# A new order table for the instructions of a fused linear-attention and MoE kernel

## The chip, the cores and the metric

The kernel runs on one core of one Trainium2 chip. The metric is device time in microseconds (us), the median of several executions. Engines: TensorE (PE; its weight loads are PEld), VectorE (DVE), ScalarE (ACT), GpSimd (POOL) and SyncE (SP), which issues all DMA transfers of this kernel.

## The reference

First a linear attention with a complex decay per channel, of which the real part goes on (4 batches, 8 heads, 768 steps, head size 48):

```
mag = np.sqrt(a_re * a_re + a_im * a_im)
scale = np.minimum(mag, 0.999) / (mag + 1e-06)
a_re_n, a_im_n = (a_re * scale, a_im * scale)
...
for t in range(S):
    ar, ai = (a_re_n[:, :, t, :, None], a_im_n[:, :, t, :, None])
    new_re = ar * S_re - ai * S_im
    new_im = ar * S_im + ai * S_re
    kv = np.einsum('bhd,bhe->bhde', k[:, :, t], v[:, :, t])
    S_re, S_im = (new_re + kv, new_im)
    y[:, :, t] = np.einsum('bhd,bhde->bhe', q[:, :, t], S_re)
```

Then, with `x` of shape (4, 768, 384) made of `y`, a gated feed-forward layer of width 1024 with a convolution of three steps:

```
h = np.maximum(x @ w_in, 0.0)
...
for k in range(K):
    conv_out += conv_w[k][None, None, :] * hp[:, k:k + S, :]
gate = 1.0 / (1.0 + np.exp(-conv_out))
return (h * gate @ w_out).astype(np.float32)
```

## The kernel before

The sequence of each batch is cut into three **segments** of two **chunks** of 128 steps, so there are 12 segments (0 to 11) and 24 chunks. The weights come in first, in eight pieces through the buffers `stk` (L278), are put together on VectorE (L248 to L251) and split into a rounded part and a rest (L281 to L287).

For each segment `prelude` loads the decay (`a_t`, L306) and works out logarithms, scans and phases on ScalarE and VectorE (L309 to L337). `products` loads `qk_t` (L345) and `v_t` (L355), takes exponentials and sines on ScalarE (L347, L348, L358, L359), and multiplies on VectorE: L349 and L350, then L360 and L361 into `qk_t`, and L362 into `a_t`. Then SyncE issues 16 DMA copies of 96 KB (L367): eight `stk<-qk_t` and eight `stk<-a_t`, one for each head, which bring real and imaginary part of a head together on 96 partitions.

For each chunk `state` turns `qk_t` (L386, L387) and adds to the running state (L393, L400), and `attention` multiplies the copies with each other in 16 matmuls (L415, in two halves), masks each half on VectorE (L419, `p_t<-ps`), and multiplies with state and values (L434, `ps<-p_t,v_t`). ScalarE takes the result (L446), VectorE the rest (L447).

The feed-forward layer works on units of 256 or 384 steps, four steps `f2` each. `moe_front`: matmul L500, ScalarE L503, VectorE L504 and L506. `moe_back`: ScalarE L518, VectorE L519, ScalarE L521, VectorE L522, matmul L527, and at a unit's end ScalarE L533 and the store L534. ScalarE's function tables are loaded where neighbouring functions need other sets (L190). A last check of the value ranges decides on a slow path, which isn't taken.

Buffers matter for loads: `a_t` has 3, `qk_t` 2, `v_t` 3 and `stk` 4, and a load or copy into a buffer waits until its last reader is done.

What sets the order: each engine executes its own list in order, and waits where an instruction's inputs or its buffer aren't ready. The lists come from the table `RANKS`, one number for each piece of work; `in_order` sorts the pieces by it and chains each engine's list. SyncE's list is the one queue in which all transfers are issued.

```
rows = pieces(list(nc.cur_bb.bb.instructions))
...
for k in sorted(range(len(rows)), key=lambda k: RANKS[k]):
    lines.setdefault(str(rows[k][0].engine), []).append(rows[k])
```

Of the kernel before, what the change touches and what calls it, by code (L numbers as in the profile page):

```python
# [47 lines left out]
    8, 13, 0, 5, 12, 11, 15, 3, 26, 7, 9, 14, 1, 4, 6, 0, 11, 21, 30, 53, 55, 69,  # L48
    72, 73, 83, 74, 82, 1, 1, 2, 3, 7, 0, 1, 9, 2, 3, 16, 3, 4, 5, 12, 14, 4,
    6, 20, 5, 9, 26, 4, 7, 8, 18, 22, 7, 8, 29, 10, 11, 34, 7, 13, 17, 20, 24, 12,  # L50
    16, 41, 13, 17, 39, 8, 25, 26, 33, 38, 18, 19, 48, 20, 21, 57, 9, 28, 31, 32, 55, 25,
    29, 67, 28, 30, 68, 13, 43, 44, 46, 70, 35, 37, 72, 36, 38, 73, 14, 45, 48, 60, 71, 40,
    48, 88, 43, 44, 91, 0, 2, 1, 0, 3, 5, 4, 6, 8, 11, 6, 11, 14, 15, 23, 10, 9,
    16, 10, 17, 19, 25, 21, 5, 18, 32, 24, 34, 6, 17, 27, 28, 27, 29, 35, 18, 16, 15, 19,
    28, 26, 25, 30, 29, 23, 24, 31, 20, 22, 21, 32, 14, 43, 15, 45, 24, 63, 22, 51, 23, 52,
    26, 2, 10, 59, 58, 27, 64, 31, 62, 32, 69, 33, 64, 34, 67, 39, 41, 78, 75, 2, 12, 19,
    23, 13, 15, 31, 33, 35, 36, 22, 36, 38, 37, 42, 30, 39, 41, 40, 46, 42, 50, 51, 12, 47,
    56, 49, 59, 27, 38, 52, 54, 54, 56, 61, 34, 47, 39, 41, 37, 35, 40, 48, 44, 49, 46, 45,
    50, 43, 42, 51, 42, 79, 45, 83, 52, 95, 46, 78, 47, 79, 49, 50, 87, 81, 102, 109, 89, 92,
    51, 98, 53, 97, 59, 107, 57, 90, 58, 92, 60, 61, 106, 98, 54, 96, 88, 96, 55, 100, 99, 101,  # L60
    56, 104, 95, 107, 62, 110, 109, 116, 64, 114, 102, 106, 66, 116, 104, 111, 121, 122, 112, 127, 115, 76,
    77, 82, 84, 67, 128, 117, 119, 68, 132, 125, 127, 130, 135, 120, 138, 123, 83, 88, 85, 92, 126, 124,
    121, 145, 131, 89, 95, 91, 97, 141, 151, 139, 155, 144, 100, 98, 103, 99, 170, 108, 172, 92, 10, 37,
    44, 50, 40, 49, 58, 60, 65, 66, 47, 62, 66, 65, 80, 53, 57, 63, 68, 76, 71, 90, 84, 36,
    77, 82, 77, 80, 52, 55, 86, 93, 84, 85, 87, 57, 60, 58, 56, 71, 66, 61, 62, 64, 70, 68,
    65, 59, 69, 67, 63, 63, 115, 65, 120, 73, 133, 69, 108, 70, 110, 71, 72, 16, 18, 125, 114, 158,
    169, 129, 131, 74, 118, 75, 122, 80, 81, 160, 147, 78, 142, 132, 137, 79, 144, 130, 134, 87, 148, 135,
    143, 90, 152, 141, 150, 93, 156, 145, 157, 94, 161, 146, 151, 154, 150, 148, 164, 152, 111, 109, 112, 114,
    96, 167, 158, 165, 102, 174, 161, 163, 162, 168, 154, 177, 159, 113, 115, 130, 126, 110, 183, 171, 187, 117,
    190, 178, 183, 178, 171, 167, 193, 177, 133, 128, 134, 132, 118, 196, 179, 184, 124, 200, 190, 191, 187, 185,  # L70
    169, 203, 188, 135, 136, 145, 147, 223, 116, 229, 137, 127, 204, 203, 205, 131, 216, 201, 211, 217, 220, 198,
    228, 207, 153, 154, 155, 157, 137, 225, 217, 229, 143, 238, 223, 224, 218, 226, 206, 232, 212, 156, 158, 163,
    160, 234, 241, 216, 247, 227, 168, 167, 172, 170, 256, 255, 232, 260, 236, 173, 181, 180, 187, 276, 156, 284,
    141, 33, 61, 74, 70, 75, 81, 85, 99, 103, 101, 76, 93, 94, 97, 111, 94, 89, 91, 86, 123, 113,
    134, 137, 53, 113, 117, 103, 105, 78, 93, 139, 140, 124, 126, 128, 73, 86, 74, 79, 75, 80, 82, 84,
    83, 85, 89, 77, 90, 87, 76, 88, 86, 157, 101, 166, 106, 180, 104, 155, 105, 156, 107, 17, 20, 181,
    164, 108, 179, 116, 189, 121, 211, 119, 172, 120, 173, 122, 123, 195, 175, 54, 105, 112, 100, 108, 118, 119,
    143, 147, 146, 129, 136, 138, 133, 159, 153, 149, 142, 140, 165, 153, 173, 175, 81, 163, 176, 162, 160, 96,
    110, 182, 184, 166, 168, 174, 98, 97, 104, 113, 95, 99, 105, 94, 102, 101, 107, 111, 109, 112, 106, 103,
    125, 207, 129, 202, 140, 215, 138, 192, 139, 193, 141, 142, 219, 197, 144, 222, 146, 224, 150, 264, 148, 202,  # L80
    149, 204, 151, 152, 19, 21, 231, 210, 252, 239, 236, 237, 159, 243, 220, 225, 161, 246, 226, 237, 165, 249,
    231, 234, 166, 254, 233, 235, 169, 262, 240, 246, 171, 263, 245, 247, 266, 268, 243, 274, 253, 186, 192, 194,
    190, 195, 196, 179, 280, 264, 275, 188, 288, 267, 282, 270, 269, 251, 282, 260, 191, 201, 203, 204, 202, 205,
    277, 278, 256, 292, 273, 208, 206, 207, 215, 216, 228, 310, 316, 290, 322, 295, 225, 226, 230, 227, 234, 231,
    329, 178, 338, 197, 341, 189, 72, 136, 188, 170, 149, 192, 191, 194, 198, 199, 176, 181, 180, 182, 205, 213,
    196, 194, 195, 221, 200, 233, 227, 100, 208, 212, 189, 214, 115, 134, 230, 240, 213, 215, 218, 121, 131, 127,
# [641 lines left out]
```

## Time and profile before

| | us |
|---|---|
| three timed executions | 421.44, 417.04, 418.19 |
| their median | 418.19 |
| the profiled execution | 414.24 |
| its span, from the first to the last instruction | 412.5 |
| busy in the span: TensorE, VectorE, ScalarE | 352.3, 326.5, 333.9 |

The rows further down come from the profiled execution, which was 3.95 us faster than the median of the timed ones. Times in rows count from the start of the span. Of the busy time of TensorE, the ends of matmuls are modelled.

### The profile page before, as it was taken

The numbers are of one execution on the slowest core, as the hardware profiler recorded it, in microseconds if no ns is written. First come the engines' busy times: TensorE is split into PE (matmuls) and PEld (weight loads), VectorE is DVE, ScalarE is ACT, GpSimd is POOL, SyncE is SP. The second block draws the span as 40 slices with busy tenths as digits, with TensorE's granted clock in tenths as the row PEclk, the third lists the DMA queues.
The fourth block names the chain that finished last, engine by engine and source line by source line (L and its number), as shares of the span: only waits on it lengthen the run. The fifth ranks groups of instructions, "written<-read, shape, count | busy, mean of one in ns | idle before, by whom it ended". The sixth has DMA issues, their size and how long they took to land.

```text
span 412.5 us, 12055 instructions
## 1 busy us (share of the span) xinstructions
PE 352.3 (85%) x5106; PEld 321.5 (78%) x5106; DVE 326.5 (79%) x515; ACT 333.9 (81%) x574; POOL 4.3 (1%) x35
## 2 busy tenths in 40 slices
PE   0566387979998979999989889799989899999993
PEld 0233365868987979998978889799979799999992
DVE  2889896669997879998998779849979778484670
ACT  5999989579998989999999979949989765453450
POOL 3000000000000000000000000000000000000000
PEclk9999798799999999999999999969999999999997
DMA  8995768284385775484768735823737533900001
GB/s 312 367 366 119 168 196 184 89 237 116 39 230 163 195 178 205 75 191 121 209 158 225 201 110 84 235 81 60 209 82 167 128 121 65 195 27 2 36 24 65
DMA packets 33231, 62.24 MB, mean 151 GB/s; under 512 B 4496, under 2 KB 26000, under 8 KB 33168
## 3 DMA queue, kind: packets, MB, share of 16 engines
q1 hardware_dynamic: 33168, 61.38, 55.5%
q8 instruction: 42, 0.69, 0.7%
q14 instruction: 21, 0.17, 0.1%
HBM read 37.77 MB, written 4.72 MB: 103 GB/s over the span
## 4 chain that ended last, share of the span: by engine, by line
PE 44%; DMA 20%; ACT 18%; DVE 6%; SPq 6%; issue 3%; ACTq 0%; DVEq 0%
PE o L527 14%; PE h_ps L500 11%; PE ps L415 7%; PE ps L434 7%; DMA qk_t<-in_qk 6%; DMA stk<-a_t 5%; DMA stk<-qk_t 5%; SPq L367 4%; ACT L190 3%; DMA v_t<-in_v 3%; PE s_ps L393 2%; PE ps L386 2%; DMA a_t<-in_a 1%; PE h_ps L285 1%; ACT h_t L503 1%
## 5 line engine op out<-in xcount | busy, mean ns | idle before, releaser
L527 PE MATMUL o<-wo,hg 128*128 128x384 f32 x576 | 116.2, 343 | 1.0 <-issue 0.8
L500 PE MATMUL h_ps<-x,wi 128*128 128x386 f32 (+1 forms) x648 | 113.0, 323 | 1.2 <-issue 1.2
L500 PEld LDWEIGHTS h_ps<-x,wi 128*128 128x128 f32 x648 | 104.0, 189 | 2.5 <-issue 1.8
L527 PEld LDWEIGHTS o<-wo,hg 128*128 128x128 f32 x576 | 98.4, 188 | 3.9 <-issue 1.2
L415 PE MATMUL ps<-stk 96*64 96x64 f32 (+1 forms) x768 | 46.0, 263 | 22.2 <-DMA stk<-a_t 9.7
L415 PEld LDWEIGHTS ps<-stk 96*64 96x64 f32 x768 | 40.0, 145 | 30.1 <-issue 10.1
L419 DVE TENSOR_TENSOR p_t<-ps,mask 128x384 f32<-128x384 f32 x48 | 26.4, 553 | 28.9 <-PE ps L415 28.2
L504 DVE SCALAR_TENSOR_TENSOR g_t<-h_t,cw 128x384 f32<-128x384 f32 (+1 forms) x72 | 40.0, 566 | 8.4 <-ACT h_t L503 8.0
L190 ACT ACT_TABLE_LOAD x36 | 46.2, 1283 | 0.6
L518 ACT ACTIVATE g_t<-g_t,cw 128x384 f32<-128x384 f32 (+1 forms) x72 | 40.0, 574 | 5.4 <-DVE g_t L506 5.3
L503 ACT ACTIVATE h_t<-h_ps 128x386 f32<-128x386 f32 (+1 forms) x72 | 31.8, 448 | 15.0 <-PE h_ps L500 15.0
L506 DVE SCALAR_TENSOR_TENSOR g_t<-h_t,cw,g_t 128x384 f32<-128x384 f32 (+1 forms) x72 | 39.9, 565 | 0.4
L285 PE MATMUL h_ps<-g_t,ident 128*128 128x384 f32 x32 | 19.9, 719 | 22.3 <-DVE g_t L251 15.0
L522 DVE TENSOR_TENSOR hg<-g_t,hg 128x768 fp32r<-128x768 f32 (+1 forms) x36 | 31.0, 861 | 5.4 <-ACT hg L521 5.4
L519 DVE SCALAR_TENSOR_TENSOR g_t<-g_t,h_t 128x768 f32<-128x768 f32 (+1 forms) x36 | 31.0, 862 | 2.0 <-ACT g_t L518 1.8
L521 ACT ACTIVATE hg<-g_t 128x768 fp32r<-128x768 f32 (+1 forms) x36 | 27.7, 769 | 5.4 <-DVE g_t L519 4.7
L434 PE MATMUL ps<-p_t,v_t 128*32 128x64 f32 x1344 | 26.9, 227 | 4.7 <-issue 4.7
L446 ACT ACTIVATE x<-ps 128x384 fp32r<-128x384 f32 x24 | 11.7, 489 | 23.6 <-PE ps L434 23.4
L434 PEld LDWEIGHTS ps<-p_t,v_t 128*32 128x32 f32 x1344 | 24.6, 115 | 6.4 <-issue 6.2
L285 PEld LDWEIGHTS h_ps<-g_t,ident 128*128 128x128 f32 x32 | 6.7, 255 | 29.1 <-issue 15.7
L434 PE MATMUL ps<-stk,s_sb 96*32 96x128 f32 x640 | 23.5, 290 | 0.1
L387 ACT COPY kn<-ps 128x512 f32<-128x512 f32 (+1 forms) x40 | 19.8, 499 | 3.8 <-PE ps L386 3.5
(93 smaller groups left out, 496.1 us busy)
## 6 DMA issues: line engine op xcount, KB each, us to landing
v_t<-in_v SPq DMA_DIRECT2D x24, 512.0 KB, 5.1
a_t<-in_a SPq DMA_DIRECT2D x12, 768.0 KB, 5.2
qk_t<-in_qk SPq DMA_DIRECT2D x12, 768.0 KB, 6.6
stk<-qk_t SPq DMA_DIRECT2D x96, 96.0 KB, 3.7
stk<-a_t SPq DMA_DIRECT2D x96, 96.0 KB, 3.7
out<-os_t SPq DMA_DIRECT2D x24, 192.0 KB, 2.8
stk<-in_w_in SPq DMA_DIRECT2D x4, 768.0 KB, 9.8
stk<-in_w_out SPq DMA_DIRECT2D x4, 768.0 KB, 6.6
```

Of the source, the lines that this page charges most:

```text
L190: row = [nc.scalar.preload_act_table_set(min(loads[k])).ins, *row]
L285: nc.tensor.matmul(rest, lhsT=ident, rhs=tmp[:, cut], start=True, stop=False)
L415: nc.tensor.matmul(sp[r0:r0 + HC, i, to], lhsT=stk[0][:, h, lo:lo + HC], rhs=stk[1][:, h, lo:], start=(i == 0 and lo == 0), stop=(i == 1 a ...
L434: nc.tensor.matmul(yp[r0:r0 + 32, q // 4, t0:t0 + right.shape[-1]], lhsT=left, rhs=right, start=r0 not in started, stop=n >= len(jobs) - H ...
L500: nc.tensor.matmul(hp, lhsT=wi[:, f2, iw, i, kt], rhs=x[ix][:, kt], start=(k == 0), stop=(k == 8))
L503: nc.scalar.activation(h, hp, func=AF.Relu)
L504: nc.vector.scalar_tensor_tensor(out=g, in0=h[:, 0:n], scalar=cw[:, f, 0:1], in1=h[:, 1:n + 1], op0=ALU.mult, op1=ALU.add)
L506: nc.vector.scalar_tensor_tensor(out=g, in0=h[:, 2:n + 2], scalar=cw[:, f, 2:3], in1=g, op0=ALU.mult, op1=ALU.add)
L518: nc.scalar.activation(g[:, i], g[:, i], func=AF.Tanh, scale=cw[:, 2 * f2 + i, 1:2])
L519: nc.vector.scalar_tensor_tensor(out=g, in0=g, scalar=1.0, in1=h[:, :, 1:n + 1], op0=ALU.add, op1=ALU.mult)
L522: nc.vector.tensor_tensor(out=lo, in0=g, in1=hi.bitcast(F32), op=ALU.subtract)
L527: nc.tensor.matmul(ops[t], lhsT=hg[:, k, t * C:(t + 1) * C], rhs=wo[:, f2, w, k], start=(f2 == 0 and hg is hi and k == 0 and w == 0), stop ...
```

## The change

Only the numbers of `RANKS` change. All 1793 pieces of work stay, with the same operands and the same buffers, but each engine's list stands in a new order. The one instruction that comes is a table load on ScalarE, which follows from the order there. The table has 82 lines; all change, and the first shows as much as any:

```
 RANKS = [
-    8, 13, 0, 5, 12, 11, 15, 3, 26, 7, 9, 14, 1, 4, 6, 0, 11, 21, 30, 53, 55, 69,
...
+    2, 10, 0, 3, 7, 8, 12, 14, 15, 6, 5, 16, 9, 0, 4, 13, 1, 0, 11, 27, 41, 58,
```

What the new numbers do is seen in the lists. A row is a line of the program, the operation, the output and the inputs (with buffer numbers), and the output's shape.

VectorE in segment 8, whose decay is `a_t_3583`: the rows up to the two L419 of its first chunk, before.

```order
L506 SCALAR_TENSOR_TENSOR g_t_3388<-h_t_3387,cw_119,g_t_3388 128x384
L522 TENSOR_TENSOR hg1_2796<-g_t_2715,hg0_2795 128x768
L504 SCALAR_TENSOR_TENSOR g_t_3388<-h_t_3387,cw_119 128x384
L519 SCALAR_TENSOR_TENSOR g_t_3360<-g_t_3360,h_t_3359 128x768
L506 SCALAR_TENSOR_TENSOR g_t_3388<-h_t_3387,cw_119,g_t_3388 128x384
L335 SCALAR_TENSOR_TENSOR a_t_4039<-a_t_4039 128x768
L419 TENSOR_TENSOR p_t_3686<-ps_3677,mask_88 128x384
L419 TENSOR_TENSOR p_t_3697<-ps_3688,mask_88 128x384
```

And now, where four more operations (L350, L319, L349, L504) stand between L335 and the first L419.

```order
L504 SCALAR_TENSOR_TENSOR g_t_3388<-h_t_3387,cw_119 128x384
L522 TENSOR_TENSOR hg1_2796<-g_t_2715,hg0_2795 128x768
L506 SCALAR_TENSOR_TENSOR g_t_3388<-h_t_3387,cw_119,g_t_3388 128x384 x2
L335 SCALAR_TENSOR_TENSOR a_t_4039<-a_t_4039 128x768
L350 TENSOR_TENSOR a_t_4039<-qk_t_4064,a_t_4039 128x768
L319 TENSOR_TENSOR a_t_4296<-a_t_4296 128x768
L349 TENSOR_TENSOR qk_t_4064<-qk_t_4064 128x768
L504 SCALAR_TENSOR_TENSOR g_t_3416<-h_t_3415,cw_119 128x384
L419 TENSOR_TENSOR p_t_3686<-ps_3677,mask_88 128x384
L519 SCALAR_TENSOR_TENSOR g_t_3360<-g_t_3360,h_t_3359 128x768
L419 TENSOR_TENSOR p_t_3697<-ps_3688,mask_88 128x384
```

Behind L335 the list before goes straight to L419; the new one does part of the next two segments' products and decay first, and an L519 comes between the two halves.

TensorE at the same place, up to the first scores of segment 8 (`ps_3677<-stk_3632,stk_3623`), before.

```order
L527 MATMUL o0_2686<-wo_118,hg1_2771 128x384 x2
L527 MATMUL o0_2686<-wo_118,hg0_2795 128x384 x4
L527 MATMUL o1_2687<-wo_118,hg1_2771 128x384 x2
L527 MATMUL o2_2688<-wo_118,hg1_2771 128x384 x2
L500 MATMUL h_ps_3430<-x0_2972,wi_117 128x386
L500 MATMUL h_ps_3430<-x1_2973,wi_117 128x386
L500 MATMUL h_ps_3430<-x0_2972,wi_117 128x386 x2
L500 MATMUL h_ps_3430<-x1_2973,wi_117 128x386
L500 MATMUL h_ps_3430<-x0_2972,wi_117 128x386 x2
L500 MATMUL h_ps_3430<-x1_2973,wi_117 128x386
L500 MATMUL h_ps_3430<-x0_2972,wi_117 128x386
L527 MATMUL o0_2686<-wo_118,hg1_2796 128x384 x2
L415 MATMUL ps_3677<-stk_3632,stk_3623 64x128
```

And now.

```order
L500 MATMUL h_ps_3430<-x1_2973,wi_117 128x386
L500 MATMUL h_ps_3430<-x0_2972,wi_117 128x386
L527 MATMUL o0_2686<-wo_118,hg0_2795 128x384 x4
L527 MATMUL o1_2687<-wo_118,hg0_2770 128x384 x4
L527 MATMUL o2_2688<-wo_118,hg1_2771 128x384 x2
L527 MATMUL o2_2688<-wo_118,hg0_2795 128x384 x4
L527 MATMUL o1_2687<-wo_118,hg1_2771 128x384 x2
L527 MATMUL o1_2687<-wo_118,hg0_2795 128x384 x4
L527 MATMUL o2_2688<-wo_118,hg1_2796 128x384 x2
L527 MATMUL o0_2686<-wo_118,hg1_2796 128x384 x2
L415 MATMUL ps_3677<-stk_3632,stk_3623 64x128
```

Twenty-four L527 stand right ahead of the scores instead of two; twelve of the 22 others stood ahead of the last L500s before (eight of them in the rows above).

SyncE's queue where segment 6 (`a_t_2826`) ends and segment 7 (`qk_t_3108`, `a_t_3083`) begins, before.

```order
L534 DMA out<-os_t_1607 128x384
L367 DMA stk_2866<-qk_t_2851 96x1x256
L306 DMA a_t_4039<-in_a 128x1536
L367 DMA stk_3123<-qk_t_3108 96x1x256 x2
L355 DMA v_t_3114<-in_v 128x1024
L367 DMA stk_3132<-a_t_3083 96x1x256
L367 DMA stk_3123<-qk_t_3108 96x1x256
L367 DMA stk_3132<-a_t_3083 96x1x256
L345 DMA qk_t_3608<-in_qk 128x1536
L355 DMA v_t_3116<-in_v 128x1024
```

And now.

```order
L355 DMA v_t_3114<-in_v 128x1024
L367 DMA stk_2875<-a_t_2826 96x1x256 x2
L367 DMA stk_2866<-qk_t_2851 96x1x256
L306 DMA a_t_4039<-in_a 128x1536
L355 DMA v_t_3116<-in_v 128x1024
L367 DMA stk_3123<-qk_t_3108 96x1x256 x3
L534 DMA out<-os_t_1610 128x384
L367 DMA stk_3132<-a_t_3083 96x1x256
L367 DMA stk_3123<-qk_t_3108 96x1x256
L345 DMA qk_t_3608<-in_qk 128x1536
```

Both loads of `v_t` for segment 7 now stand ahead of its copies, and the second (`v_t_3116`) takes the buffer that L434 of segment 6's first chunk reads.

## Rows read from the trace of the kernel before

**Rows 1.** The page's head: the span of the profiled execution.

```profile
span 412.5 us, 12055 instructions
```

**Rows 2.** Busy time by stage: stretch, length, busy us of each engine, clock, DMA.

```profile
47.60:322.00 274.40, 251.08 (x4070) 233.79 (x4070) 234.56 (x373) 247.70 (x431) 1.08 (x15) 0.97 0.62 155
322.00:412.50 90.50, 81.97 (x1000) 79.04 (x1000) 55.84 (x93) 43.62 (x84) 0.00 (x0) 0.97 0.27 71
```

**Rows 3.** Waits, 47.6 to 330 us: who waited for whom, us, times, longest.

```profile
PE ps L415 <- DMA stk<-a_t: 9.7, 10, 1.8
...
PE ps L415 <- DMA stk<-qk_t: 5.5, 3, 2.9
```

**Rows 4.** Line 367, the copies: SyncE's ns each (min/median/max), and landing.

```profile
L367 SPq DMA_DIRECT2D stk<-qk_t x96: 571/594/1662, 34.0 to 355.8; - x96
...
DMA to landing us min/median/max: 2.7/3.7/8.0
```

**Rows 5.** Timeline of VectorE, segment 8: start, us, what, idle before.

```profile
244.11 0.95 DVE L519 SCALAR_TENSOR_TENSOR g_t<-g_t,h_t 128x768 f32<-128x768 f32 x1
244.98 0.95 DVE L319 TENSOR_TENSOR a_t<-a_t 128x768 f32<-128x768 f32 x1
...
250.60 0.61 DVE L504 SCALAR_TENSOR_TENSOR g_t<-h_t,cw 128x384 f32<-128x384 f32 x1
251.13 1.75 DVE L362 TENSOR_TENSOR a_t<-a_t 128x1536 f32<-128x1536 f32 x1
...
270.21 0.56 DVE L419 TENSOR_TENSOR p_t<-ps,mask 128x384 f32<-128x384 f32 x1 [4.10 <-PE ps L415]
```

**Rows 6.** Timeline of TensorE: idle time before L415 in segments 1, 6 and 8.

```profile
68.96 1.97 PE L415 MATMUL ps<-stk 96*64 96x128 f32 x24 [1.64 <-DMA stk<-a_t]
71.99 0.87 PE L415 MATMUL ps<-stk 96*64 96x128 f32 x6 [1.06 <-DMA stk<-a_t]
...
211.30 1.66 PE L415 MATMUL ps<-stk 96*64 96x128 f32 x32 [0.84 <-DMA stk<-a_t]
...
268.66 2.79 PE L415 MATMUL ps<-stk 96*64 96x128 f32 x30 [2.89 <-DMA stk<-qk_t]
```

**Rows 7.** The same timeline, twelve L527 in a row ahead of segment 8.

```profile
257.78 2.33 PE L527 MATMUL o<-wo,hg 128*128 128x384 f32 x12
```

**Rows 8.** The page's clock in 40 slices (tenths), and the stretch behind segment 8's gap.

```profile
PEclk9999798799999999999999999969999999999997
...
267.80:274.60 6.80, 5.94 (x120) 5.77 (x123) 1.98 (x3) 1.53 (x3) 0.00 (x0) 0.50 0.38 121
```

**Rows 9.** Timeline of VectorE: idle before L419, segments 4, 6, 7, 9, 10.

```profile
153.50 1.23 DVE L419 TENSOR_TENSOR p_t<-ps,mask 128x384 f32<-128x384 f32 x2 [1.87 <-PE ps L415]
...
212.34 0.56 DVE L419 TENSOR_TENSOR p_t<-ps,mask 128x384 f32<-128x384 f32 x1 [0.85 <-PE ps L415]
...
234.70 0.56 DVE L419 TENSOR_TENSOR p_t<-ps,mask 128x384 f32<-128x384 f32 x1 [2.51 <-PE ps L415]
...
303.93 1.23 DVE L419 TENSOR_TENSOR p_t<-ps,mask 128x384 f32<-128x384 f32 x2 [2.44 <-PE ps L415]
...
324.06 1.23 DVE L419 TENSOR_TENSOR p_t<-ps,mask 128x384 f32<-128x384 f32 x2 [1.03 <-PE ps L415]
```

**Rows 10.** Line 190, ScalarE's table loads: ns each.

```profile
L190 ACT ACT_TABLE_LOAD  x36: 1283/1283/1283, 7.3 to 335.3; - x36
```

**Rows 11.** Waits of SyncE's queue: the longest in total.

```profile
SPq L367 <- DVE qk_t L361: 67.6, 8, 14.3
```

**Rows 12.** Timeline of SyncE, segment 6: its first copies and the next transfer.

```profile
187.39 2.22 SPq L367 DMA_DIRECT2D stk<-qk_t  x3
196.59 0.35 SPq L534 DMA_DIRECT2D out<-os_t  x1
```

**Rows 13.** Timelines: L434 of segment 6's first chunk, and segment 7's first copies.

```profile
213.60 1.20 PE L434 MATMUL ps<-p_t,v_t 128*32 128x64 f32 x55
...
216.78 1.21 SPq L367 DMA_DIRECT2D stk<-qk_t  x2
```

## What the new order will do to the time, predicted before it ran

> **What bounds the kernel now.** I read the page's head and the busy time by stage first, then the waits, then one stall on every engine that stands in it. The span is 412.5 us and the profiled execution 414.24 us, so 1.7 us lie around the span; the median of the three timed runs is 418.19 us, 3.95 us above that execution. I make the sum on 414.24 and add 3.95 at the end [rows 1]. The stages differ. From the first score matmul at 47.6 us to the last segment's at 322 us, TensorE is busy 251.1 of 274.4 us, ScalarE 247.7 and VectorE 233.8; after 322 us TensorE is busy 82.0 of 90.5 us and the others about half [rows 2]. So the tail is TensorE's own work, which a new order can't shorten, and the prize is the 23.3 us that TensorE stands in the middle stage, with the time up to 47.6 us, in which ScalarE and VectorE work through the first segment's decay.
>
> In the middle stage 15.2 us of the 23.3 are one kind of wait: L415, the scores, for the DMA copies `stk<-a_t` (9.7 us) and `stk<-qk_t` (5.5 us) [rows 3]. Each segment (0 to 11, two chunks each) has one such round trip: VectorE's L361 and L362 make the products, SyncE issues 16 copies of 96 KB, L415 reads them, VectorE's L419 masks the scores, L434 reads those, and ScalarE's L446 takes the result. The trip is long because of the copies: 594 ns of SyncE for each, so 16 take about 9.5 us, and 2.7 to 8.0 us more to land [rows 4]. Whatever each engine has in its order between its ends of this trip is cover; what the trip takes beyond it is a stall of all three. Segment 8 shows it: L362 starts at 251.13 us, VectorE runs out of other work and stands 4.10 us before L419 at 270.21 [rows 5], TensorE stands 2.89 us before L415 at 268.66 [rows 6].
>
> **The change part by part.** No instruction goes and one comes: a 37th table load on ScalarE counting those of L190, all else is moved. To weigh a move I add up the start-to-start times of the rows that stand between two instructions of one engine, in each order: 0.87 us for a 768-wide VectorE operation (244.11 to 244.98 us), 0.53 for a 384-wide L504 (250.60 to 251.13) [rows 5], 0.19 for an L527 (12 in 2.33 us) [rows 7].
>
> *Cover of the copies.* In segment 8 VectorE's list between L362 and L419 gains three L504, one L350, one L319 and one L349 and loses one L519: 3 x 0.53 + 3 x 0.87 - 0.87 = 3.3 us, against 4.10 us of standing there. On TensorE 22 more L527 stand between the last L500 and the first L415; twelve of them stood ahead of that L500 before, so ten are new ahead of L415, 10 x 0.19 = 1.9 us. L362 itself has 1.1 us less VectorE work ahead of it: 3.0 us of slack against the gap of 2.89. Counted in the same way (TensorE's work ahead of the first L415, less VectorE's up to the end of L362), the slack grows in segments 2 to 10 by 1.1, 1.6, 2.8, 1.9, 0.6, 1.9, 3.0, 3.6 and 3.4 us. Of the 15.2 us, segment 1 has 1.64 + 1.06 = 2.7; the other 12.5 are closed but for rests of 0.15 and 0.24 us in segments 3 and 6 (gap 0.84), where the gap is longer than the slack gained [rows 6]. Term: **-12.1 us**. Bounds: 0 and -12.5.
>
> *The clock.* [...] The other gaps of segments 2 to 10 left the clock up, so without this gap I expect it to stay; the work then takes half: 5.94 / 2 = **-3.0 us** (bounds 0 and -3.0).
>
> *L419 behind more work.* What covers the copies on VectorE also stands ahead of L419. Where that is more than VectorE's idle time there, L419 comes late, and TensorE waits at L434 instead, which it never did on VectorE before. VectorE's list between L362 and L419 grows by 3.6, 2.2, 2.5, 3.1, 3.3, 5.0 and 3.6 us in segments 4 to 10; its idle time at that place was 1.87, none, 0.85, 2.51, 4.10, 2.44 and 1.03 us [rows 5, 9]. The excess is 1.7 + 2.2 + 1.6 + 0.6 + 0 + 2.6 + 2.6 = 11.3 us. That is one end; the other is 0, since VectorE stands 40.6 us in the middle stage, twice what is named here, and L362 comes earlier as well [rows 2]. I take a third, nearer to zero because the trace has no wait of L434 for L419 at all: **+3.8 us**.
>
> *The start.* Segment 1's L415 has 2.6 us less TensorE work ahead of it, while its L361, from which the copies start, comes only 1.4 us earlier: TensorE stands longer there, **+1.2 us**. Segment 0's copies start at the same point of VectorE's work: before, L251 freed their buffer after L361; now L251 is done earlier and L361 is 2.8 us later, which cancels to 0.1 us. The weight loads are reshuffled too, and I allow 1.5 us either way.
>
> *Table load.* One more at 1283 ns [rows 10]. ScalarE stands 274.4 - 247.7 = 26.7 us in the middle stage [rows 2], mostly waiting for L434, and that covers it; without the cover it would cost 1.3 us. I take 0.
>
> *SyncE's queue.* Between the first and the last copy of a segment stand 25 other transfers in all segments together, 32 before; at 0.4 to 0.6 us of issue each that is no loss. But loads and stores now stand right ahead of a segment's first copy at three places; that is the second rival.
>
> *Buffers.* SyncE's wait before the copies is for L361, 67.6 us in 8 waits [rows 11], not for a free `stk` buffer. [...]
>
> **Sum.** 414.24 - 12.1 - 3.0 + 3.8 + 1.2 = 404.1 us, and with 3.95 us **408 us** as a median.
>
> **The rivals.** *First, the wait changes places:* the L415 gaps close, and all 11.3 us come back at L434, TensorE still stands at the same points of the trip, and the clock still falls: 414.24 - 12.1 + 11.3 + 1.2 = 414.6, a median of 418.6 us. For it: in segments 5, 9 and 10 VectorE had little idle time left to fill. Against it: VectorE's whole idle time.
>
> *Second, slower: SyncE stands ahead of the copies.* In the new queue a `v_t` load stands ahead of the first copy of segments 4 and 7 and an `out` store ahead of that of segment 9. The load of segment 7 waits for TensorE to finish the L434 of segment 6; before, it stood behind three copies. SyncE works its list in order, so a late L434 or L533 now holds all 16 copies. The trace has such a stand: in segment 6 three copies go out from 187.39 for 2.22 us and then SyncE does nothing until the store at 196.59, 7.0 us [rows 12]. At half of that in three segments, with a third of the 12.1 us lost with them: 414.24 - 8.1 - 3.0 + 3.8 + 1.2 + 10.5 = 418.6, a median of 423 us; at the full 7.0 us, 433. It decides from 2.0 us at each (6.1 us of gain over three). Against it: L434 of segment 6 ended at 213.60 + 1.20 = 214.8 us [rows 13] and the copies of segment 7 went out only at 216.78, 2.0 us later.
>
> *Third, the order isn't what holds the copies* (buffers, as above, or transfers that share the DMA engines and land late anyway): the gaps stay, the start's term remains, 415.4, a median of 419.4 us. For it: a copy may take 8.0 us to land instead of 2.7 [rows 4].
>
> **How the numbers follow.** About 1% is what a measurement of this kernel can tell from no change; 1% of 418.19 is 4.2 us. Forecast 0.56, first rival 0.20, second 0.14, third 0.10. Faster by over 1% (under 414.0): the forecast and a sliver of the first rival, 0.57. Within 1%: most of the first and the third, 0.27. Slower: the second and the bad ends of the others, 0.16. The range: all of both gains and none of the costs is 414.24 - 15.1 = 399.1, 403.1 as a median, less 1.5 for the start, 401.6; above, it takes in the first and third rivals and the near edge of the second, 422. The forecast's own range is 402 to 414.
>
> **What would show it.** Right: waits of L415 for `stk` under 5 us instead of 15.2, VectorE's at L419 well under what they were, a clock of 1.00 at the first scores of segment 8, and waits of L434 for L419 of some 4 us. The first rival would show as L434 waiting 8 us or more for L419; the second as SyncE's wait at L355 or L534 for TensorE or ScalarE, with the copies right behind; the third as the same L415 waits with the same releasers. The prediction fails above all if TensorE, arriving earlier everywhere, meets VectorE and ScalarE that have no slack left: then gaps appear at L500 and L527, where the trace has nearly none.

## The result, and the profile after

| | before | after |
|---|---|---|
| median of five timed executions, us | 417.85 | 395.89 |
| lowest to highest, us | 415.62 to 421.44 | 394.90 to 397.87 |
| the profiled execution, us | 414.24 | 397.85 |
| its span, us | 412.5 | 396.1 |
| mean granted clock of TensorE | 0.969 | 0.982 |

The new order takes 0.947 of the time (95% interval 0.941 to 0.953): 22.0 us less between the medians, 16.4 us between the profiled executions. The forecast was 408 us, in a range from 401.6 to 422; the time lies below it.

The page of the new kernel: span, the clock in 40 slices (tenths), then groups with busy time, mean ns of one, idle time before them and its main releaser.

```profile
span 396.1 us, 12054 instructions
...
PEclk9999997999899999999999999999999999999997
...
L190 ACT ACT_TABLE_LOAD x37 | 47.5, 1283 | 0.6
...
L415 PE MATMUL ps<-stk 96*64 96x128 f32 (+1 forms) x768 | 40.4, 257 | 2.3 <-issue 2.0
...
L419 DVE TENSOR_TENSOR p_t<-ps,mask 128x384 f32<-128x384 f32 x48 | 26.1, 551 | 7.2 <-PE ps L415 6.8
```

TensorE no longer waits for a copy at L415: the 15.2 us of [rows 3] are gone. The waits of the new kernel from segment 0's first scores to 330 us (who for whom: us, times, longest) say the same for the rest of the trip:

```profile
ACT x L446 <- PE ps L434: 6.7, 5, 2.5
...
DVE p_t L419 <- PE ps L415: 6.1, 8, 1.8
PE ps L434 <- issue: 5.5, 4, 2.5
...
PE ps L434 <- DVE p_t L419: 1.0, 4, 0.3
```

VectorE stood 22.9 us at L419 in that stretch before, and ScalarE 19.3 us at L446. Now the busy time by stage, as in [rows 2]: from segment 0's first scores to those of segment 10, and from there on.

```profile
46.40:306.30 259.90, 248.81 (x4039) 230.67 (x4033) 233.82 (x372) 246.26 (x431) 1.37 (x14) 0.98 0.67 167
306.30:396.10 89.80, 81.01 (x995) 78.15 (x994) 54.15 (x90) 45.13 (x87) 0.00 (x0) 0.98 0.22 62
```

The middle stage went from 274.4 to 259.9 us, and TensorE's idle time in it from 23.3 to 11.1 us. The tail kept its length. (322 us, which the prediction calls the last segment's first scores, is segment 10's.) The chain of work that ended last, followed back, has moved from TensorE and the transfers to ScalarE. Its shares of the span by engine, before and after:

```profile
PE 44%; DMA 20%; ACT 18%; DVE 6%; SPq 6%; issue 3%; ACTq 0%; DVEq 0%
```

```profile
ACT 44%; PE 33%; DMA 10%; DVE 5%; issue 4%; SPq 2%; ACTq 0%; POOL 0%; DVEq 0%
```

To place the gain I use one number for a point of the program, its **lost time**: the start of a segment's scores, less TensorE's work ahead of them in its own list, at one duration for each kind of matmul (0.174 us for an L527, 0.176 for an L500 of 386 columns, and so on, from the trace before). A stall adds to it, and so does work at a lower clock (the same 22 L415 take 1.22 us at a clock of 1.00 and 2.18 at 0.50, see e12); a mere reordering doesn't. For segments 4 and 8 it stands for both chunks.

| first scores of segment | 0 | 1 | 2 | 4 | 8 | 10 | end of TensorE |
|---|---|---|---|---|---|---|---|
| before | 33.3 | 35.5 | 44.4 | 48.8, 51.0 | 57.0, 63.1 | 66.5 | 67.7 |
| after | 32.6 | 36.6 | 38.1 | 43.4, 43.1 | 47.0, 47.2 | 48.6 | 51.2 |
| before, second profile (e12) | 33.3 | 34.9 | 45.1 | 50.0, 56.0 | 64.8, 68.8 | 72.1 | 73.5 |
| e1: new up to segment 2 | 32.7 | 35.1 | 36.0 | 41.4, 46.6 | 56.2, 62.8 | 65.6 | 66.8 |
| e2: old up to segment 2 | 32.4 | 34.5 | 44.9 | 52.4, 52.2 | 55.5, 55.7 | 56.9 | 59.9 |
| e4: new in segments 7 and 8 | 33.1 | 34.6 | 45.3 | 50.2, 56.1 | 61.8, 62.0 | 64.7 | 66.5 |
| e7: ten L527 moved | 32.6 | 34.6 | 43.7 | 47.6, 52.9 | 58.7, 60.5 | 65.0 | 67.7 |

Between the first two rows lie 16.5 us: 6.3 up to segment 2, 3.7 from there to segment 8, 5.9 within segment 8 and 0.6 behind it (2.0 up to segment 10's first scores, of which 1.4 are lost again in the tail). Columns 1 and 2 have to be taken together: a stall of TensorE of 2.5 to 2.9 us that waits for nothing in the profile ("issue", see the last section) lies behind segment 1's first scores before, and ahead of them in the new kernel. Segment 8 on TensorE in the new kernel, and the stretch around its scores:

```profile
252.82 4.33 PE L527 MATMUL o<-wo,hg 128*128 128x384 f32 x24
257.08 1.56 PE L415 MATMUL ps<-stk 96*64 96x128 f32 x32
...
256.90:262.00 5.10, 5.10 (x186) 4.69 (x184) 5.10 (x9) 5.04 (x8) 0.00 (x0) 1.00 0.01 3
```

The 24 L527 run into the scores without the 2.89 us of [rows 6], and the clock stays at 1.00 where [rows 8] has 0.50. The start, up to segment 2, holds the gain that was not forecast, and segment 1 most of it. VectorE's timeline there, of the kernel before (first wait of the program, L361 and L362 of segment 1), then of the new one:

```profile
7.34 0.96 DVE L311 SCALAR_TENSOR_TENSOR a_t<-a_t,e_t 128x768 f32<-128x768 f32 x1 [7.34 <-ACT a_t L309]
...
52.80 0.96 DVE L361 TENSOR_TENSOR qk_t<-qk_t,a_t 128x768 f32<-128x768 f32 x1
...
57.26 1.75 DVE L362 TENSOR_TENSOR a_t<-a_t 128x1536 f32<-128x1536 f32 x1
```

```profile
5.44 0.18 DVE L248 TENSOR_SCALAR ct<-cd 128x24 int32<-128x24 int32 x1 [5.44 <-DMA cd<-in_conv_w]
...
47.22 0.96 DVE L361 TENSOR_TENSOR qk_t<-qk_t,a_t 128x768 f32<-128x768 f32 x1
...
49.95 1.75 DVE L362 TENSOR_TENSOR a_t<-a_t 128x1536 f32<-128x1536 f32 x1
```

L361 comes 5.6 us earlier and L362 7.3 us, so the copies have landed (65.3 us instead of 71.9) when TensorE reaches L415 at 65.4. TensorE's work and clock over segments 0 and 1, before and after:

```profile
47.60:95.30 47.70, 40.48 (x754) 34.07 (x754) 35.17 (x61) 38.61 (x70) 0.00 (x0) 0.87 0.66 167
```

```profile
46.40:89.10 42.70, 38.55 (x717) 31.91 (x711) 32.34 (x55) 38.89 (x72) 0.00 (x0) 0.92 0.75 173
```

The new stretch has 37 matmuls fewer in it (717 for 754), so its 1.9 us less of busy time are not the clock's alone. Where the clock differs is at segment 0's first scores. TensorE's last long stand ahead of them and the clock behind it, before:

```profile
47.62 3.52 PE L415 MATMUL ps<-stk 96*64 96x128 f32 x32 [6.14 <-ACT a_t L358]
...
47.60:52.50 4.90, 4.81 (x80) 4.23 (x80) 4.22 (x8) 4.88 (x7) 0.00 (x0) 0.50 0.51 152
```

And after:

```profile
43.11 1.65 PE L285 MATMUL h_ps<-g_t,ident 128*128 128x384 f32 x2 [4.63 <-ACT wi L287]
...
46.40:51.40 5.00, 4.69 (x102) 3.73 (x97) 4.55 (x6) 4.98 (x8) 0.00 (x0) 1.00 0.64 192
```

The comparisons with the kernel before below are of medians of all executions (23, 17 and 11 of the kernel before, beside e1 to e4, e5 to e8 and e9 to e12): its times spread from 409 to 423 us, and the ratio that goes with a run leaves out what is over 1.5% above a kernel's fastest execution, which here cuts away 34 of the 51 of the kernel before.

| | median, us | lowest to highest | executions | kernel before beside it |
|---|---|---|---|---|
| e1: new order up to segment 2 | 415.05 | 413.35 to 419.70 | 12 | 418.30 |
| e2: old order up to segment 2 | 404.87 | 400.79 to 406.52 | 6 | 418.30 |
| e3: only SyncE's list new | 423.16 | 420.30 to 428.21 | 6 | 418.30 |
| e4: new order in segments 7 and 8 | 413.94 | 411.15 to 416.76 | 12 | 418.30 |
| e5: old order in segments 7 and 8 | 409.10 | 405.85 to 411.57 | 6 | 416.16 |
| e6: VectorE's and ScalarE's lists of e4 | 427.83 | 422.69 to 431.87 | 6 | 416.16 |
| e7: ten L527 moved | 416.19 | 411.91 to 420.04 | 12 | 416.16 |
| e8: SyncE's list old from segment 2 on | 410.31 | 402.05 to 412.50 | 6 | 416.16 |
| e9: only loads and copies old there | 404.28 | 401.07 to 406.86 | 6 | 417.68 |
| e10: only stores old there | 408.70 | 406.35 to 413.57 | 6 | 417.68 |
| e11: one store moved ahead | 397.27 | 393.29 to 399.02 | 6 | 417.68 |
| e12: the kernel before | 419.40 | 418.74 to 420.05 | 2 | 417.68 |

### The profile page after: what moved, and what is told of

It is laid out like the page before. It is cut to its first block, busy times and chain, and to the rows that moved or that the text cites. A ratio compares the mean times of both kernels' runs of the same rounds, so it can differ in the third digit from the quotient of the medians.

```text
span 396.1 us, 12054 instructions
## 1 busy us (share of the span) xinstructions
PE 349.9 (88%) x5106; PEld 318.9 (81%) x5106; DVE 326.1 (82%) x515; ACT 334.0 (84%) x575; POOL 4.6 (1%) x35
## 4 chain that ended last, share of the span: by engine, by line
ACT 44%; PE 33%; DMA 10%; DVE 5%; issue 4%; SPq 2%; ACTq 0%; POOL 0%; DVEq 0%
PE o L527 12%; PE h_ps L500 10%; ACT L190 7%; PE ps L434 4%; PE ps L415 4%; ACT g_t L518 3%; DMA stk<-a_t 3%; ACT h_t L503 3%; DMA out<-os_t 2%; DMA qk_t<-in_qk 2%; SPq L367 2%; ACT kn L387 2%; ACT hg L521 2%; ACT a_t L309 2%; ACT a_t L358 2%
## 5 line engine op out<-in xcount | busy, mean ns | idle before, releaser
L527 PE MATMUL o<-wo,hg 128*128 128x384 f32 x576 | 117.6, 345 | 1.0 <-ACT os_t L533 0.5
L500 PE MATMUL h_ps<-x,wi 128*128 128x386 f32 (+1 forms) x648 | 115.2, 325 | 1.0 <-ACT x L446 0.7
L500 PEld LDWEIGHTS h_ps<-x,wi 128*128 128x128 f32 x648 | 105.3, 191 | 3.1 <-issue 1.1
L527 PEld LDWEIGHTS o<-wo,hg 128*128 128x128 f32 x576 | 99.2, 189 | 3.6 <-issue 0.7
L415 PEld LDWEIGHTS ps<-stk 96*64 96x64 f32 x768 | 36.1, 141 | 8.8 <-issue 5.5
L504 DVE SCALAR_TENSOR_TENSOR g_t<-h_t,cw 128x384 f32<-128x384 f32 (+1 forms) x72 | 39.8, 565 | 3.9 <-ACT h_t L503 3.6
L415 PE MATMUL ps<-stk 96*64 96x128 f32 (+1 forms) x768 | 40.4, 257 | 2.3 <-issue 2.0
L285 PE MATMUL h_ps<-g_t,ident 128*128 128x384 f32 x32 | 20.2, 731 | 23.3 <-DVE g_t L251 12.7
L519 DVE SCALAR_TENSOR_TENSOR g_t<-g_t,h_t 128x768 f32<-128x768 f32 (+1 forms) x36 | 30.9, 861 | 10.0 <-ACT g_t L518 10.0
L521 ACT ACTIVATE hg<-g_t 128x768 fp32r<-128x768 f32 (+1 forms) x36 | 27.6, 771 | 7.8 <-DVE g_t L519 5.2
L434 PE MATMUL ps<-p_t,v_t 128*32 128x64 f32 x1344 | 27.0, 220 | 6.2 <-issue 5.5
L419 DVE TENSOR_TENSOR p_t<-ps,mask 128x384 f32<-128x384 f32 x48 | 26.1, 551 | 7.2 <-PE ps L415 6.8
L434 PEld LDWEIGHTS ps<-p_t,v_t 128*32 128x32 f32 x1344 | 23.5, 109 | 8.7 <-issue 6.6
L285 PEld LDWEIGHTS h_ps<-g_t,ident 128*128 128x128 f32 x32 | 7.1, 262 | 28.3 <-ACT wi L287 14.2
L434 PE MATMUL ps<-stk,s_sb 96*32 96x128 f32 x640 | 22.1, 277 | 0.5 <-DVE p_t L419 0.5
L533 ACT ACTIVATE os_t<-o 128x384 f32<-128x384 f32 x24 | 11.8, 490 | 12.7 <-PE o L527 6.3
L386 PE MATMUL ps<-ident,qk_t 128*128 128x128 f32 x120 | 20.6, 288 | 1.5 <-DVE x L447 1.5
```

The costliest lines, as they stand in the source:

```text
L415: nc.tensor.matmul(sp[r0:r0 + HC, i, to], lhsT=stk[0][:, h, lo:lo + HC], rhs=stk[1][:, h, lo:], start=(i == 0 and lo == 0), stop=(i == 1 a ...
L434: nc.tensor.matmul(yp[r0:r0 + 32, q // 4, t0:t0 + right.shape[-1]], lhsT=left, rhs=right, start=r0 not in started, stop=n >= len(jobs) - H ...
L500: nc.tensor.matmul(hp, lhsT=wi[:, f2, iw, i, kt], rhs=x[ix][:, kt], start=(k == 0), stop=(k == 8))
L504: nc.vector.scalar_tensor_tensor(out=g, in0=h[:, 0:n], scalar=cw[:, f, 0:1], in1=h[:, 1:n + 1], op0=ALU.mult, op1=ALU.add)
L519: nc.vector.scalar_tensor_tensor(out=g, in0=g, scalar=1.0, in1=h[:, :, 1:n + 1], op0=ALU.add, op1=ALU.mult)
L521: nc.scalar.activation(hi, g, func=AF.Copy)
```

## The experiments

The theory of the forecast is that the gain is cover: work put between the copies and their readers closes the L415 gaps of segments 2 to 10 and saves the low clock (0.50) behind one, segment by segment, while the start costs a little. The rivals after the result are that the start pays, that SyncE's order (earlier loads and copies) pays, and that the parts don't add up at all. Only numbers of `RANKS` change in all kernels; where many do, one line of the table is shown. An old or new order "up to segment 2" means all instructions that start ahead of segment 2's first L415 in that order; the rest follows in the other order.

### e1 and e2: the start

e1, against the kernel before (28 lines):

```diff
-    77, 82, 84, 67, 128, 117, 119, 68, 132, 125, 127, 130, 135, 120, 138, 123, 83, 88, 85, 92, 126, 124,
+    77, 82, 84, 67, 129, 118, 120, 68, 133, 126, 128, 131, 122, 121, 138, 124, 83, 88, 85, 92, 127, 125,
```

> The new order up to the first scores (L415) of segment 2, the old order from there on. Theory from the two traces (the start pays: TensorE no longer stands 6.14 us ahead of segment 0's scores, its clock stays up behind them, and segment 1's two gaps are gone): about 6 us faster than before, some 412 us, and the gap and the low clock at segment 8 are still there. Theory of the forecast (the start costs 1.2 us, all gain lies in segments 2 to 10): 419 us, 0 to 2 us slower than before.

e2, against the new kernel (24 lines):

```diff
-    48, 90, 51, 93, 56, 115, 54, 82, 55, 84, 57, 58, 109, 97, 59, 102, 92, 95, 60, 104, 96, 98,
+    51, 98, 53, 97, 59, 107, 57, 90, 58, 92, 60, 61, 106, 98, 54, 96, 88, 96, 55, 100, 99, 101,
```

> The other half: the old order up to the first scores (L415) of segment 2, the new order from there on. Theory that the start pays 6 us: about 10 us faster than before (408 us), and 5 to 7 us slower than the whole new order. Theory of the forecast: at least as fast as the whole new order (395 to 396 us), since the start costs it 1.2 us.

e1 took 415.05 us, 3.3 less than the kernel before, half of what the start theory said; e2 took 404.87, 9.0 us more than the whole new order, more than it said. The ratios to the kernel before are 1.004 (0.998 to 1.010) and 0.975 (0.964 to 0.987). e2 decides against the forecast's theory: an old start is not worth 1.2 us but costs 9. e1 doesn't decide: its ratio can't be told from no change, and only the medians show its 3.3 us. The profiles agree with e2: up to segment 2 it has lost 6.8 us more than the whole new kernel. The table of lost time tells why the two halves differ: e1 reaches segment 2 at 36.0, 8.4 us better than before, and ends at 66.8, 0.9 better. The old order behind it takes the head start back. e1's timeline of TensorE, its stalls for VectorE and copies:

```profile
92.09 1.10 PE L434 MATMUL ps<-stk,s_sb 96*32 96x128 f32 x32 [3.61 <-DVE p_t L419]
...
146.97 1.26 PE L415 MATMUL ps<-stk 96*64 96x128 f32 x22 [3.60 <-DMA stk<-qk_t]
...
232.52 2.54 PE L415 MATMUL ps<-stk 96*64 96x128 f32 x32 [3.54 <-DMA stk<-qk_t]
...
268.48 2.79 PE L415 MATMUL ps<-stk 96*64 96x128 f32 x30 [3.52 <-DMA stk<-qk_t]
```

The first is at the seam of the two orders. The others stand where the kernel before stalled for 2.21, 1.44 and 2.89 us, and are longer: TensorE comes earlier, the copies hardly do. As these rows read, the round trip and not TensorE sets the pace of the old order there, and a head start of TensorE ends as waiting. With the new order behind it the same start keeps its 6 us.

### e3: SyncE's list alone

Against the kernel before (45 lines, SyncE's numbers only):

```diff
-    110, 182, 184, 166, 168, 174, 98, 97, 104, 113, 95, 99, 105, 94, 102, 101, 107, 111, 109, 112, 106, 103,
+    94, 182, 184, 166, 168, 174, 97, 100, 105, 102, 98, 108, 96, 111, 104, 109, 106, 101, 107, 110, 103, 112,
```

> Only SyncE's list is the new one; TensorE, VectorE, ScalarE and GpSimd keep the old order. Theory that cover on TensorE and VectorE makes the gain: within 2 us of before (416 to 420 us), with waits of L415 for stk of 13 us or more in the stretch from 47.6 to 330 us. Rival, that copies and loads issued further ahead make it: 5 us or more faster (under 413 us), with those waits under 8 us. Rival, that the new queue stands at v_t loads and out stores ahead of copies: slower by 3 us or more.

423.16 us, 4.9 more than the kernel before (ratio 1.020, 1.009 to 1.030): the third expectation, slower. Not by a stand of SyncE at loads and stores, though. e3's timelines of SyncE, VectorE and TensorE in segment 2:

```profile
88.74 0.38 SPq L345 DMA_DIRECT2D qk_t<-in_qk  x1
```

```profile
95.22 0.96 DVE L349 TENSOR_TENSOR qk_t<-qk_t 128x768 f32<-128x768 f32 x1 [8.46 <-DMA qk_t<-in_qk]
```

```profile
98.75 1.95 PE L434 MATMUL ps<-stk,s_sb 96*32 96x128 f32 x32 [7.72 <-DVE p_t L419]
```

The new queue issues the `qk_t` load of segment 3 behind segment 2's copies, at 88.74 us instead of 78.61. VectorE's old list has the L349 that reads it ahead of segment 2's L419, and stands 8.46 us; TensorE stands 7.72 us behind it. The queue is right for the new lists only.

### e4 to e7: segment 8

e4, against the kernel before (26 lines; all engines):

```diff
-    384, 279, 396, 275, 346, 276, 347, 277, 278, 391, 349, 280, 351, 281, 358, 285, 286, 401, 363, 292, 407, 380,
+    378, 280, 398, 278, 349, 279, 351, 281, 282, 394, 356, 283, 355, 287, 360, 288, 289, 406, 365, 294, 410, 389,
```

> The new order on all engines only between the first scores of segment 7 and those of segment 9, the old order before and behind. Theory of the forecast, cover and clock: the 2.89 us gap of segment 8 closes and the clock stays up behind it, 5.9 us together, so some 412 us. Rival, that the wait only changes places or that the clock falls elsewhere: under 2 us faster.

e5 is the same exchange against the new kernel, the other way round (25 lines):

```diff
-    378, 280, 398, 278, 349, 279, 351, 281, 282, 394, 356, 283, 355, 287, 360, 288, 289, 406, 365, 294, 410, 392,
+    384, 279, 396, 275, 346, 276, 347, 277, 278, 391, 349, 280, 351, 281, 358, 285, 286, 401, 363, 292, 407, 380,
```

> The new order everywhere but between the first scores of segment 7 and those of segment 9, where the old order stands. Theory that segment 8's cover is worth its gap and its clock by itself: about 5.9 us slower than the whole new order, some 402 us, with TensorE standing 2 us or more ahead of the first L415 of segment 8. Rival, that the head start of the new order behind segment 7 hides the gap: under 398.5 us, and no wait of L415 for stk there.

e6 takes only VectorE's and ScalarE's numbers of e4 (25 lines):

```diff
-    384, 279, 396, 275, 346, 276, 347, 277, 278, 391, 349, 280, 351, 281, 358, 285, 286, 401, 363, 292, 407, 380,
+    378, 279, 398, 275, 349, 276, 351, 277, 278, 394, 356, 280, 355, 281, 360, 285, 286, 406, 365, 292, 410, 389,
```

> The old order, but VectorE's and ScalarE's lists are the new ones between the first scores of segment 7 and those of segment 9; TensorE's and SyncE's lists stay old. Theory that the covers on VectorE and TensorE add up: L362 comes some 1 us earlier, TensorE's gap ahead of segment 8's L415 falls from 2.89 to about 1.8 us, VectorE's idle time at L419 from 4.10 to about 1 us, and the whole gains 1 to 2 us (about 416.5 us) with the clock still falling. Rival, that VectorE's and ScalarE's order alone does it: 413 us or less, as with all lists.

e7, as TensorE's list (5 lines of the table); the three rows are taken out behind segment 8's scores:

```diff
 L527 MATMUL o0_2686<-wo_118,hg1_2796 128x384 x2
+L527 MATMUL o2_2688<-wo_118,hg0_2795 128x384 x4
+L527 MATMUL o1_2687<-wo_118,hg0_2795 128x384 x4
+L527 MATMUL o2_2688<-wo_118,hg1_2796 128x384 x2
 L415 MATMUL ps_3677<-stk_3632,stk_3623 64x128
```

> The old order with one edit: the ten L527 that the new order has ahead of segment 8's first L415 and the old one behind it are put right ahead of it. Theory of the forecast: 1.9 us of the 2.89 us gap is filled, the start of L415 stays where it is, and with a gap of 1 us the clock stays up: 4.9 us faster, some 413.4 us. Rival, that the clock still falls behind the shorter gap: 1.9 us faster, some 416.4 us.

e4 is 4.4 us faster than the kernel before by the medians, though its ratio, 0.999 (0.992 to 1.006), doesn't tell it from no change. Its trace does, in the place itself: segment 8 loses 0.2 us instead of 6.1, and TensorE's timeline has the 24 L527 right ahead of the scores, with no idle time:

```profile
271.90 1.56 PE L415 MATMUL ps<-stk 96*64 96x128 f32 x32
```

Behind segment 8 e4 loses 4.5 us, as the kernel before does (4.6): this gain stays. e5 confirms the price at the place, and adds another. Its timeline of TensorE:

```profile
263.64 2.36 PE L415 MATMUL ps<-stk 96*64 96x128 f32 x30 [3.57 <-DMA stk<-qk_t]
...
303.68 1.96 PE L434 MATMUL ps<-p_t,v_t 128*32 128x64 f32 x56 [4.28 <-DVE p_t L419]
```

The gap of segment 8 is back (ratio to the kernel before 0.989, 0.983 to 0.995), and its lost time goes from 51.3 to 56.9, 5.6 us. The rest of the 13.2 us over the whole new order lies elsewhere, above all in 4.28 us at the seam behind it, where L419 stands behind too much work on VectorE: the first rival's mechanism, seen where two orders meet. e6 and e7 take the engines apart. With VectorE's and ScalarE's lists alone the kernel is 11.7 us slower (ratio 1.028, 1.019 to 1.036), against both expectations:

```profile
294.60 3.45 PE L500 MATMUL h_ps<-x,wi 128*128 128x386 f32 x9 [5.34 <-ACT x L446]
```

Ahead of it ScalarE stands for 7.3 us at an L521 that waits for an L527 which TensorE's old list has later, and L446 stands behind it. The ten L527 alone do in the trace what was forecast for them: the gap is 1.19 us and the clock stays at 1.00, so segment 8 loses 1.8 us instead of 6.1.

```profile
270.45 1.52 PE L415 MATMUL ps<-stk 96*64 96x128 f32 x30 [1.19 <-DMA stk<-qk_t]
...
321.63 2.59 PE L415 MATMUL ps<-stk 96*64 96x128 f32 x32 [1.85 <-DMA stk<-a_t]
```

And still the median is that of the kernel before, 416.19 against 416.16 (ratio 1.003, 0.997 to 1.008). Both expectations were of a gain, and fail. In the profiled execution 7.2 us are lost behind segment 8 instead of 4.6: the waits for copies in segments 9 and 10 (0.74 and 1.85 us) are no longer than before, but 1.3 us of "issue" come at 276.8 us, and the clock is at 0.50 from 321.9 to 325.3, behind segment 10's gap (in the first profile of the kernel before it stayed at 1.00 behind a gap of 1.81 us at the same place). Whether that is chance or follows from the edit, one profile can't tell; why segment 8's gain on TensorE alone doesn't reach the median stays open.

### e8 to e10: SyncE's list in the new order

e8, against the new kernel (30 lines, SyncE's numbers from segment 2 on):

```diff
-    138, 297, 299, 275, 273, 154, 159, 304, 305, 277, 280, 282, 162, 172, 176, 165, 160, 161, 173, 169, 175, 177,
+    144, 297, 299, 275, 273, 161, 166, 304, 305, 277, 280, 282, 160, 167, 176, 159, 171, 163, 172, 173, 175, 162,
```

> The new order on all engines, but SyncE's list is the old one from segment 2 on. Theory that cover on the engines makes the gain and the queue's order none: within 2 us of the whole new order (394 to 398 us). Rival, that earlier issue of loads and copies carries part of it: 400 us or more, with waits of L415 for stk back.

e9 (24 lines) keeps the new places of the stores:

```diff
-    330, 324, 323, 331, 332, 337, 447, 244, 451, 249, 456, 264, 137, 283, 301, 284, 290, 296, 315, 318, 321, 320,
+    330, 324, 323, 331, 332, 337, 447, 244, 451, 249, 456, 264, 135, 283, 301, 284, 290, 296, 315, 318, 321, 320,
```

> The new order on all engines; in SyncE's list from segment 2 on the loads and copies stand in the old order, and each out store stands behind as many of them as in the new one. Theory that the old queue costs 14 us through its stores (ScalarE's L533 waits for an os_t buffer, and L446, L500 wait behind it): back to 394 to 399 us, and ScalarE waits for out stores no longer than the 6.3 us of the whole new order. Rival, that the order of loads and copies carries it: 406 us or more.

e10 (24 lines) keeps the new order of loads and copies:

```diff
-    138, 297, 299, 275, 273, 154, 159, 304, 305, 277, 280, 282, 162, 172, 176, 165, 160, 161, 173, 169, 175, 177,
+    138, 297, 299, 275, 273, 154, 160, 304, 305, 277, 280, 282, 163, 172, 176, 165, 161, 162, 173, 169, 175, 177,
```

> The complement: the new order on all engines, in SyncE's list the loads and copies in the new order and each out store behind as many of them as in the old one. Theory of the stores: 406 us or more, with ScalarE waiting over 9 us for out stores. Rival of the loads: 394 to 399 us.

e8 costs 14.4 us over the new kernel (ratio to the kernel before 0.979, 0.969 to 0.989, where the new kernel has 0.947): my theory of cover on the engines alone falls. But the waits of L415 for copies, which the rival named, are not back (0.9 us). e9 and e10 split it: old loads and copies cost 8.4 us, old stores 12.8, together more than e8. e9's 404.28 us lies between its two sides. e10 has the time that the theory of the stores gave, but not its sign: ScalarE's total wait for stores doesn't follow the time (6.3 us in the new kernel, 7.8 in e9, 5.5 in e10). A single stand does. ScalarE, SyncE and TensorE in e10:

```profile
266.82 0.53 SPq L534 DMA_DIRECT2D out<-os_t  x1
```

```profile
270.18 0.49 ACT L533 ACTIVATE os_t<-o 128x384 f32<-128x384 f32 x1 [4.13 <-DMA out<-os_t]
```

```profile
275.43 2.65 PE L500 MATMUL h_ps<-x,wi 128*128 128x386 f32 x9 [3.51 <-ACT x L446]
```

In the new kernel the same L533 waits 1.32 us, and the store that frees its `os_t` buffer is out ahead of segment 9's copies:

```profile
262.86 0.35 SPq L534 DMA_DIRECT2D out<-os_t  x1
```

In e10 the store stands behind two copies that wait for L361. ScalarE stands 4.13 us, L446 is late behind it, TensorE stands 3.51 us at L500 and the clock behind it is at 0.50 (276.9 to 280.3 us): from segment 8's second scores to segment 9's first 5.8 us are lost instead of 1.4. e8 has the same stall, 2.95 us, and a second one of the same kind in the tail, ScalarE's first and then TensorE's:

```profile
388.56 0.49 ACT L533 ACTIVATE os_t<-o 128x384 f32<-128x384 f32 x1 [3.39 <-DMA out<-os_t]
```

```profile
389.11 14.00 PE L527 MATMUL o<-wo,hg 128*128 128x384 f32 x62 [3.11 <-ACT os_t L533]
```

The clock is at 0.50 from 390 to 394 us behind it, and from segment 10's first scores to the end this execution loses about 6 us more than the new kernel. It took 411.68 us, and e8's six spread from 402.05 to 412.50, so the second stall needn't be in all of them. In e9 the copies are late again at one place, segment 7:

```profile
223.92 1.22 PE L415 MATMUL ps<-stk 96*64 96x128 f32 x24 [2.59 <-DMA stk<-a_t]
```

The rest of e10 and e9 is not traced to single places.

### e11: a version that might beat both

Against the new kernel, as SyncE's list:

```diff
 L534 DMA out<-os_t_2823 128x384
+L534 DMA out<-os_t_3574 128x384
 L355 DMA v_t_4827<-in_v 128x1024
 L345 DMA qk_t_4821<-in_qk 128x1536
-L534 DMA out<-os_t_3574 128x384
```

> The new order with one edit in SyncE's list: the out store of os_t_3574, issued at 303.99 us behind a v_t and a qk_t load and 6.2 us on its way, stands ahead of both. Theory that ScalarE's stand of 2.83 us at 310.3 us lies on the path that ends last: 1 to 2.8 us faster than the whole new order, 393 to 395 us. Rival, that TensorE's slack of the last segments hides it: 396 us, within 1 us.

ScalarE's stand of 2.83 us is gone in the trace, and the time, 397.27 us, is that of the new kernel within what can be told. The theory's gain doesn't come, and the rival's reason fits the trace: TensorE hardly waited for that stand (0.47 us at an L527 in the new kernel).

### e12: the kernel before once more

No edit.

> The kernel before, unchanged, for a second profile. Theory that the clock falls behind segment 4's gap in most executions of the old order and that the first profile was one in which it didn't: from the first to the second chunk's scores of segment 4 TensorE loses over 5 us against its work instead of 2.2, the granted clock there is 0.50 for some us, and the execution takes 416 us or more. Rival, that the spread comes from elsewhere (the start, the DMA transfers): 2 to 3 us lost there, as in the first profile.

The second profile is of an execution of 420.05 us. Segment 4 on TensorE in it, with the stretch behind, and then the same in the first profile:

```profile
155.19 2.18 PE L415 MATMUL ps<-stk 96*64 96x128 f32 x22 [3.29 <-DMA stk<-qk_t]
...
154.20:161.00 6.80, 5.81 (x130) 5.59 (x134) 3.06 (x5) 2.64 (x6) 0.00 (x0) 0.50 0.60 202
```

```profile
152.91 1.22 PE L415 MATMUL ps<-stk 96*64 96x128 f32 x22 [2.21 <-DMA stk<-qk_t]
...
153.00:160.00 7.00, 7.00 (x195) 6.55 (x197) 5.84 (x10) 5.57 (x14) 0.16 (x3) 1.00 0.56 190
```

A gap of 3.29 us instead of 2.21, and the clock at 0.50 behind it: segment 4 loses 6.0 us instead of 2.2. e1, e4 and e7, which have the old order there, lose 5.2, 5.9 and 5.3. So the first profile was of an execution that kept its clock at this place, and the theory holds there. It is not the whole spread. Of the 5.8 us between the two spans (412.5 and 418.3) segment 4 makes 3.8; the second profile also has the clock at 0.50 at 90, 128 and 242 us, where the first has it at 1.00, and loses less in segment 8 (4.0 us instead of 6.1). And e1, e4 and e7 were profiled in executions of 413.35, 412.91 and 414.14 us, no slower than the first profile's 414.24, with segment 4's low clock in them.

## Why the prediction was wrong, point by point

The direction, the place of the waits and the three mechanisms were right: cover closes the gaps, the clock comes with them (1.00 instead of 0.50 at segment 8), L419 moves behind more work. Two steps of the sum failed, and they make more than the whole miss of 12 us: the start was forecast at +1.2 us and gave -6.3, which is 7.5, and the 3.95 us between profile and median were added to both kernels, where the new one has -1.96 (395.89 less 397.85), which is 5.9. The other terms, -11.3 in sum, measured -10.2.

*The start (+1.2 us).* Failed. I counted that L361 of segment 1 has 1.4 us less work ahead of it on VectorE. It came 5.6 us earlier. The other 4 us are waits that I didn't count: up to L361 VectorE stood some 11.8 us before and 8.0 us after, among them 1.34 us at segment 1's L335, which are gone, and 1.23 us for the convolution's weights, which the new list takes at the program's first instruction, where VectorE stands in either order (6.7 us in two waits ahead of the first L311 instead of 7.3). TensorE stood 6.14 us right in front of segment 0's scores before; now it stands 4.63 us, weight matmuls (L285) come between, and the scores run at a clock of 1.00 instead of 0.50; the 4.81 us of work in the slow stretch would be some 2.4 us at the full clock, an estimate from its row. The mean granted clock over segments 0 and 1 is 0.92 instead of 0.87. And segment 1's two gaps, 2.7 us, which I kept, went. e2 shows that the gain belongs to the start, and e1's trace that it needs the new order behind it.

*The added 3.95 us.* Failed. I took the difference between the first profile and the median as a constant of the measurement. It was the chance of which execution was profiled: the new kernel's profile lies on the other side of its median. e12 shows where a difference of that size can come from: at segment 4 the first profile lost 2.2 us with the clock up, and four others with the old order there (e1, e4, e7, e12), behind gaps of 2.5 to 3.6 us, 5.2 to 6.0 with the clock at 0.50. The new order has no gap there. But that this stall makes the 3.95 us or the spread is not shown: over the 51 executions of the kernel before the mean granted clock hardly goes with the time (0.936 at the fastest, 409.16 us, and 0.954 at 418.76). The five executions of the new kernel lie within 3.0 us of each other, the five of the kernel before beside them within 5.8, and the 51 later ones within 13.8.

*Cover (-12.1 us) and L419 (+3.8).* Right in the mechanism, and near in the sum, which is partly luck. From segment 2 to segment 8 the terms were -5.9 for gaps and +2.0 for L419, and 3.7 us were measured. L434 waits 1.0 us for L419 in the whole new kernel, not four, so this term was near its end at zero, and the gaps gave less than their length; the two misses, some 3 and 4 us, have opposite signs. Behind segment 8 the forecast was -1.6 and -0.6 came. Segments 2 to 7 were not tried by themselves: that cover made their 3.7 us is read from the traces.

*The clock at segment 8 (-3.0).* Right. The term is half of the 5.94 us of work at a clock of 0.50 in [rows 8]; no run shows it apart from the gap. Gap and clock together were to give 5.9 us there, and the lost time says 5.9; e4 and e5 give 5.9 and 5.6 at the same place.

*The table load (0).* Nothing speaks against it: ScalarE stands 0.6 us ahead of table loads in both. It was not tried by itself.

*SyncE's queue.* The stand of the second rival is there: SyncE waits 12.8 us in three waits at `v_t` loads for L434. It costs nothing, since it ends as L361 does: the copies of segment 4 go out with the end of L361 at 127.8 us, those of segment 7 0.8 us behind it. What I missed is that the queue can hurt through its other readers, `qk_t` loads in e3 (VectorE stands 8.46 us) and stores in e8 (ScalarE stands 7.0 us in two waits) and e10 (4.13 us).

*Buffers.* They don't explain the waits at L415, and the third rival fell: the buffers are the same, and the 15.2 us are gone.

*Adding up.* From segment 2 on the sum over places came near for the whole order, and not for pieces of it. These gave 3.3 (e1), 4.4 (e4), 0 (e7), -4.9 (e3) and -11.7 us (e6) of gain: where one engine's list or one half is changed, waits at the next take the gain back (e1) or more (e3, e6).

## What to carry to other kernels

The lists of the engines are one object: move work on all engines that take part in a round trip, and judge a stretch by the time lost in it, not by a gap closed on one engine. To say when a moved instruction will run, add up the waits ahead of it as well as the work, from the start of the program. And a profile is one execution: before its distance from the median is added to a forecast, take a second profile, and look for stalls behind which the clock falls in one and not in the other, as it did here at segment 4 (0.50 and 1.00).

## What the runs showed of the hardware that was not expected

TensorE's longest stalls with the releaser "issue" lie at instruction numbers of one series in both orders. Counted over all instructions of its queue in the trace (weight loads, matmuls and the semaphore instructions between them), those at L434, L500 and L527 come at numbers 1473, 2753, 4545, 5313 and 6081 in the kernel before and 705, 1985 (an L415), 2753, 4545 and 6081 in the new one: all are 193 more than a multiple of 256. The two longest, before and after:

```profile
88.64 0.44 PE L434 MATMUL ps<-p_t,v_t 128*32 128x64 f32 x13 [2.87 <-issue]
```

```profile
62.75 0.42 PE L434 MATMUL ps<-p_t,v_t 128*32 128x64 f32 x8 [2.50 <-issue]
```

The page's table of DMA queues has two of the kind "instruction"; the larger of them:

```profile
q8 instruction: 42, 0.69, 0.7%
```

Its packets are 0.69 MB / 42 = 16.4 KB each. In the 14 traces of this study such stalls of 0.25 us or more sum to 3.7 to 11.7 us each, most of it within rows of short matmuls (L434: 4.7 us before, 5.5 after); one alone lasts 3.49 us (e4). What TensorE waits for in them was not shown, nor whether these queues have to do with it: no run took the stalls away. They are as long in both orders, 7.3 us before and 7.8 after. What follows them isn't: behind the new kernel's stalls at 62.75 and 96.72 us the mean granted clock is 0.50 (65.3 to 70.9 us) and 0.68 (96.7 to 101.0), behind the 2.87 us of the kernel before it is 1.00 (88.6 to 93.0). What they cost in all was not worked out.
